# Attention with its gradient: one small turn taken from the DMA queue to TensorE, zero rows stored later, GpSimd's table spread over more steps

## Chip, cores and metric

One core of a Trainium2 chip. The metric is the device time of the whole program in microseconds (us), lower is better. The kernel computes a gated mix of an attention block and a state-space convolution and all its gradients, in bfloat16 with sums in float32.

## The reference, cut to what matters

The forward function is below; the kernel must return its output and the gradients with respect to all inputs but `B_u`, for a given `grad_out` of 1 x 2048 x 576 (32 heads of 18, 2048 positions).

```python
def _A_ref(x, wqkv, wo):
    qkv = (x @ wqkv).reshape(B, S, 3, H, Dh).transpose(2, 0, 3, 1, 4)
    q, k, v = qkv[0], qkv[1], qkv[2]
    scores = jnp.einsum("bhqd,bhkd->bhqk", q, k) * (Dh ** -0.5)
    p = _softmax(scores, axis=-1)
    o = jnp.einsum("bhqk,bhkd->bhqd", p, v)
    return o.transpose(0, 2, 1, 3).reshape(B, S, D) @ wo
...
x = A_x
g = _sigmoid((x * gate_w).sum(-1, keepdims=True))
a = _A_ref(x, A_wqkv, A_wo)
b = _B_ref(x, ...)   # a convolution over the sequence with a kernel made of 128 complex powers per channel
return g * a + (1 - g) * b
```

## The kernel before

The program has four parts: projections and preparations (to about 205 us in the profile), attention forward and backward (to about 2200 us), the convolution part, and the last products. All three parts of the change lie in the attention part.

**Units and steps.** Heads are taken in 8 groups `g` of four, queries in 4 blocks `b` of 512. A pair (g, b) is a *unit*: 32 units, numbered u = 4g + b. A loop over `G` walks through steps, 32 (`NST`) to a unit; below, "step s of unit u" is G = 32u + s. The step range of the forward part is `NTOT` = 1024. The backward part of a unit runs `OFF` = 39 steps behind its forward part: it begins at step 7 of the next unit. So the backward part of a new group begins at step 7 of units 1, 5, 9, ... 29.

**One step.** The order of every engine's instructions is written out by hand in this loop, and each engine runs its own list in order. First come the actions put on record for the step (`at(("pre", G), ...)`: loads and stores). TensorE then makes a pair of score tiles for the forward part (P1), does the "burst" of the step, a pair of score tiles for the backward part (P3), and a pair of products of V with the gradient (P2, named `ps_P<-dOaT,VaT_g` in the profile). ScalarE takes the exponentials of P1 (`PT`, line 780) and of P3 (`eb`, line 785), 128 x 1024 each. VectorE multiplies each P2 tile with its PT into `ds` (line 790).

**Bursts.** They go by `slot`, the place of the step in eight: two steps each for the sums of dV, dQ and dK (`dv_half`, `dq_half`, `dk_half`; the second step of each ends with an addition on VectorE, `gb` when it is the last of its sum), and two slots, 4 and 7, in which `turn_ds` turns blocks of `ds` on TensorE. All bursts share one PSUM bank, `accB`, so a burst waits until VectorE has emptied the one before.

**Turned copies of ds.** dK needs `ds` turned, as `dsT`. For each 128 keys, SyncE issues a DMA transpose for three of the four heads (line 798); the fourth is turned by TensorE and copied by VectorE (lines 561 and 562). `by_pe(p)` says how many of the two tiles of pair p are treated so: none for p = 5, one for p = 6, else both; where TensorE doesn't, the DMA transpose takes all four heads.

**The end of a unit's forward part.** At step 0 of the next unit the sum `accO` is complete and copied (f0, line 500). At step 2 (f1) TensorE turns it, VectorE takes the reciprocals `rl` of the softmax sums and the normalised output `Ob`, and GpSimd scales the gradient with the reciprocals into `dOa` (line 514) and multiplies it with Ob into `prod` (line 516). At step 3 (f2) VectorE reduces prod into the last column of each head's part of `dOa` (line 522), and SyncE stores Ob (line 523) and turns `dOa` into `dOaT` (line 525). P2 reads dOaT from step 7 on, and dV's burst reads dOa.

**SyncE's queue.** It holds all loads of attention, the DMA transposes of ds, dOaT, and those of finished gradients: `store_grad` turns a `gb` into `gT` (line 534), which GpSimd packs and stores (lines 538 and 539). `gb` has two buffers, so the third next sum waits until a gT has landed. In the last unit of a group (b = 3) the sums of dV and dK end for each of the four key blocks, so that eight gT come on top of dQ's one.

**GpSimd.** It builds the table `E_d` of complex powers for the convolution (lines 358 to 420: products of two small tables, stored 144 times by GpSimd's own DMAs) in pieces between its other work. `e_emit(G)` issues as many pieces as `want` says for the step, except in steps 0 and 1 of a unit. It also copies rows of x and of the gated gradient into layouts for the convolution (`put_x`, `put_gy`, every 56 steps from G = 78 and 98), and stores zero rows: one DMA into `Kp_d` at G = 40, and seven (`put_zero`, line 681) into `xb_d` at G = 46, 50, ... 70. The convolution part, after attention, reads all of these.

Of the kernel before, what the change touches and what calls it, by code (L numbers as in the profile page):

```python
# [11 lines left out]
BF = mybir.dt.bfloat16  # L12
# [5 lines left out]
P = 128  # L18


def build(tc, aps, dbg_aps=None, stages=("s1", "attn", "post", "s4", "final")):
    nc = tc.nc
# [39 lines left out]
    with ExitStack() as gctx:  # L62
# [3 lines left out]
        ident_bf = const.tile([P, P], BF, name="ident_bf")  # L66
# [37 lines left out]
        Kp_d = dram.tile([NBLK, 2 * P, CB], BF, name="Kp_d")  # L104
# [11 lines left out]
        with ExitStack() as ctx:  # L116
            s1 = ctx.enter_context(tc.tile_pool(name="s1", bufs=1))
            work = ctx.enter_context(tc.tile_pool(name="s1work", bufs=2))
# [310 lines left out]
        if "attn" in stages:  # L429
            KB = 512  # L430
            NQ = S // KB
            TPQ = KB // P
            DA = HP
            NFILL = {"V": 1, "Q": 0, "K": 0}
            with ExitStack() as ctx:
# [3 lines left out]
                work = ctx.enter_context(tc.tile_pool(name="awork", bufs=2))  # L439
                apsp = ctx.enter_context(tc.tile_pool(name="aps", bufs=1, space=bass.MemoryType.PSUM))  # L440
# [39 lines left out]
                UN = {}  # L480
# [13 lines left out]
                def post_forward(g, b, acc):  # L494
                    U = UN[(g, b)]
                    st = {}

                    def f0():
                        st["oT"] = work.tile([P, KB], F32, tag="oT", bufs=1, name="oT")
                        nc.vector.tensor_copy(st["oT"], acc)  # L500

                    def f1(po):
                        for qi in range(TPQ):
                            nc.tensor.transpose(po[:, qi * P:(qi + 1) * P], st["oT"][:, qi * P:(qi + 1) * P], ident_f)
                        po = po.rearrange("p (t a b) -> p t a b", a=4, b=HP)

                        def ev():
                            rl = work.tile([P, TPQ, 4], F32, tag="rl", bufs=1, name="rl")
                            nc.vector.reciprocal(rl, po[:, :, :, DH])
                            rlb = rl.unsqueeze(3).to_broadcast([P, TPQ, 4, DH])  # L510
                            Ob = st["Ob"] = work.tile([P, TPQ, 4, DH], BF, tag="Ob", bufs=1, name="Ob")
                            nc.vector.tensor_tensor(Ob, po[:, :, :, 0:DH], rlb, op=A.mult)
                            da = U["dOa"]
                            nc.gpsimd.tensor_tensor(da[:, :, :, 0:DH], U["dO"], rlb, op=A.mult)
                            prod = st["prod"] = work.tile([P, TPQ, 4, DH], F32, tag="oT", bufs=1, name="prod")
                            nc.gpsimd.tensor_tensor(prod, da[:, :, :, 0:DH], Ob, op=A.mult)
                        return ev

                    def f2():
                        da, Ob, prod = U["dOa"], st["Ob"], st["prod"]  # L520
                        with nc.allow_low_precision(reason="summed in float32 by the engine, rounded once when written"):
                            nc.vector.tensor_reduce(da[:, :, :, DH], prod, axis=AX.X, op=A.add, negate=True)
                        nc.sync.dma_start(O_d[:, b * TPQ:(b + 1) * TPQ, 4 * g * DH:4 * (g + 1) * DH], Ob.rearrange("p t a b -> p t (a b)"))
                        U["dOaT"] = work.tile([P, TPQ, P], BF, tag="dOaT", name="dOaT")
                        nc.sync.dma_start_transpose(out=U["dOaT"], in_=U["dOa"].rearrange("p t a b -> p (t a b)"))
                    return f0, f1, f2

                def grad_tile():
# [22 lines left out]
                def by_pe(p):  # L551

                    return {NPF: 0, NPF + 1: 1}.get(p, 2)

                def turn_ds(U, p):

                    n = by_pe(p)
                    pt_ = apsp.tile([P, n, TPQ, P], BF, tag="accB", name="dst_p")
                    for x in range(n):
                        for qb in range(TPQ):  # L560
                            nc.tensor.transpose(pt_[:, x, qb, :], U["ds"][2 * p + 2 - n + x][:, 3, qb * P:(qb + 1) * P], ident_bf)  # L561
                    return lambda: nc.vector.tensor_copy(U["dsT", p][:, 2 - n:2, 3 * TPQ:, :], pt_)  # L562

                NPF = 5
                NST = 2 * NT
                NU = NG * NQ
                OFF = NST + 7
                units = [(g, b) for g in range(NG) for b in range(NQ)]
# [3 lines left out]
                def at(n, f):  # L572
                    todo.setdefault(n, []).append(f)

                def accB(name):
                    return apsp.tile([P, KB], F32, tag="accB", name=name)
# [3 lines left out]
                def fill(acc, n, w=4):  # L580
                    o_ = acc[:, (4 - w) * P:4 * P].rearrange("p (a b) -> p a b", b=P)
                    for _ in range(n):
                        mm(o_, lhsT=J_bf, rhs=fill_r[:, 0:w, :])
# [57 lines left out]
                e_total = sum(x[0] for x in eops)  # L641
                e_done = [0.0, 0]

                def e_emit(G):

                    want = (e_total + 270.0) * min(1.0, max(0.0, (G - 10) / (NTOT - 40)))
                    while e_done[1] < len(eops) and e_done[0] < want:
                        e_done[0] += eops[e_done[1]][0]
                        eops[e_done[1]][1]()
                        e_done[1] += 1  # L650
# [15 lines left out]
                NTOT = NU * NST  # L666
# [13 lines left out]
                def put_zero(r):  # L680
                    nc.gpsimd.dma_start(xb_v[:, :, r, :].rearrange("b k w -> k b w"), zrow[:, 0:SUB * CB].unsqueeze(1).to_broadcast([NB, NBLK, SUB * CB]))

                at(("pre", 40), lambda: nc.gpsimd.dma_start(Kp_d[:, 0:P, :].rearrange("b (z u) c -> b z (u c)", z=2),
                                                            zrow.unsqueeze(1).to_broadcast([NBLK, 2, S])))
                for r in range(NSUB - 1):
                    at(("pre", 46 + 4 * r), lambda r=r: put_zero(r))
                for k in range(NT):
                    at(("pre", 78 + 56 * k), lambda k=k: put_x(k))
                    at(("pre", 98 + 56 * k), lambda k=k: put_gy(k))
                for G in range(NTOT + OFF + 24):  # L690
# [4 lines left out]
                    if G < NTOT:  # L695
                        u, s = divmod(G, NST)
                        g, b = units[u]
# [11 lines left out]
                    if r1:  # L709
                        g, b, i, j0 = r1  # L710
# [5 lines left out]
                    evs = []  # L716
                    slot = (G2 + 1) % 8
                    m_ = (G2 - (7, 8, 8, 8, 8, 8, 8, 0)[slot]) // 8
                    if ("f1", G) in todo:
                        acc = accB("accF")  # L720
                        evs.append(todo.pop(("f1", G))[0](acc))
                        e_done[0] += 1.4
                    elif 0 <= m_ < NTOT // 8:
                        u_, kq = divmod(m_, NQ)
                        g, b = units[u_]
                        if slot in SLOTS:
                            nm, burst, h = SLOTS[slot]
                            if h == 0:
                                acc = accB("acc" + nm)
                                fill(acc, NFILL[nm])  # L730
                                burst(g, b, kq, 0, acc)
                            else:
                                evs.append(burst(g, b, kq, 1, acc))
                                if nm == "Q" and kq == NQ - 1:
                                    at(("pre", G + 2), lambda g=g, b=b: store_grad(UN[(g, b)].pop("dqa"), g, 0, b * TPQ))
                                elif nm in "KV" and b == NQ - 1:
                                    at(("pre", G + 2), lambda g=g, kq=kq, nm=nm: store_grad(DKV.pop((nm.lower(), g, kq)), g, 1 + "KV".index(nm), kq * TPQ))
                        elif by_pe(2 * kq + (slot == 4)):
                            evs.append(turn_ds(UN[(g, b)], 2 * kq + (slot == 4)))
                    if r2:  # L740
                        g, b, s2 = r2
                        T = grp_t[g]
                        U = UN[(g, b)]
                        par_ = (s2 + OFF) % 2
                        jo = 2 * par_
                        kq, ii = s2 // 8, (s2 % 8) // 2
# [11 lines left out]
                    if G % 8 in (0, 3, 4, 7) and G >= 3:  # L758
                        i_ = (G - 3) // 8 * 4 + {3: 0, 4: 1, 7: 2, 0: 3}[G % 8]
                        u_, i_ = divmod(i_, NT)  # L760
                        if 0 <= u_ < NU:
                            g, b = units[u_]
# [13 lines left out]
                    for (kind, g, b, i, j, ps) in rows:  # L776
                        U = UN[(g, b)]
# [8 lines left out]
                        else:  # L786
# [6 lines left out]
                            if U["dsn", i] == nj:  # L793
                                p = i // 2
                                assert j == nj - 1
                                if i % 2 == 0:
                                    U["dsT", p] = work.tile([P, 2, 4 * TPQ, P], BF, tag="dsT", bufs=3, name="dsT")
                                nc.sync.dma_start_transpose(out=U["dsT", p][:, i % 2, 0:nj * TPQ, :],
                                                            in_=U["ds"][i][:, 0:nj, :].rearrange("p j q -> p (j q)"))
# [5 lines left out]
                    if G % NST not in (0, 1) or G >= NTOT:  # L805
                        e_emit(G)
# [359 lines left out]
        if "final" in stages and "s4" in stages:  # L1166
# [14 lines left out]
            with ExitStack() as ctx:  # L1181
# [128 lines left out]
                work = ctx.enter_context(tc.tile_pool(name="pbwork", bufs=2))  # L1310
# [5 lines left out]
                for t in range(NT):  # L1316
                    if t % TB == 0:
                        OT4 = work.tile([P, TB, DC, P], BF, tag="OT4", name="OT4")
                        nc.sync.dma_start_transpose(out=OT4.rearrange("p t c q -> p (t c) q"),
                                                    in_=O_tok[:, t:t + TB, :].rearrange("p t d -> p (t d)"))  # L1320
# [100 lines left out]
```

## Time and profile before

| | |
|---|---|
| time, median of three runs | 2997.47 us (2994.35 to 3002.66) |
| span of the profiled execution | 2998.7 us |
| attention: first and last exponential | 205.2 and 2198.3 us |
| exponentials, PT and eb | 1024 each, 128 x 1024 |
| DMA transposes of ds | 512 |
| DMA transposes of dOa | 32, 1.20 us of SyncE each (median) |
| stores of zero rows into xb_d | 7 of 288 KB, at 266.6 to 312.8 us |

How to read it: in the lists of instructions a line has the start in us, the duration in us, the engine, the line of the kernel, the operation, and `out<-in` by the program's names with the shapes; `x2` means two instructions merged. Brackets at the end give the idle time of that engine just before, and what ended it. `SPq` is SyncE's queue of DMA issues, where a duration is that of issuing, not of the transfer. In the table of stretches a row begins with the stretch and its length, and each engine has its busy time. The DMA share is the mean busy share of the 16 DMA engines; where packets overlap it can exceed 1.

### The profile page before, as it was taken

Reading aid. Unit: us, or ns where it says so; the run is one execution under the profiler, and the core shown is the slowest. Engines: PE = TensorE matmul, PEld = TensorE weight load, DVE = VectorE, ACT = ScalarE, POOL = GpSimd, SP = SyncE. Lnnn points to the kernel's source line nnn. Section 1 sums busy time; section 2 is a strip of 40 time slices with the busy share of each in tenths; the row PEclk is TensorE's granted clock in tenths of the full one; section 3 lists DMA queues with packets and bytes.
Section 4 is the critical chain, followed back from the end, with each engine's and each line's share of the span. In section 5 each row is a group of like instructions: output and inputs, shape, how many; then the busy total and the mean of one; then the engine's idle time right before and its main releaser. Section 6 shows DMA issues by size and latency. Waiting matters only on the chain.

```text
span 2998.7 us, 69333 instructions
## 1 busy us (share of the span) xinstructions
PE 2484.7 (83%) x27004; PEld 1188.0 (40%) x27004; DVE 2350.2 (78%) x4115; ACT 2374.2 (79%) x2765; POOL 1606.3 (54%) x2653
## 2 busy tenths in 40 slices
PE   4768888888988888888888898888947878886679
PEld 2432232332333233233233233323226777776447
DVE  4436797898889888898889888988836888889634
ACT  2449898999999899999999999999736777675111
POOL 1038888888888799888888888850010000000010
PEclk8877798999999899999999999999757878887889
DMA  8857999989989989989998999997688887872886
GB/s 223 159 151 123 155 160 164 165 160 168 162 158 164 163 157 167 167 160 161 176 154 164 168 167 154 165 166 127 122 189 215 210 198 207 213 190 72 245 207 130
DMA packets 1310750, 504.17 MB, mean 168 GB/s; under 512 B 1205182, under 2 KB 1280544, under 8 KB 1301204
## 3 DMA queue, kind: packets, MB, share of 16 engines
q1 hardware_dynamic: 1281908, 439.11, 76.5%
q0 software_dynamic: 20624, 53.26, 7.5%
q10 hardware_dynamic: 7888, 7.38, 0.8%
q8 instruction: 211, 3.46, 0.5%
q14 instruction: 119, 0.97, 0.1%
HBM read 144.48 MB, written 99.69 MB: 81 GB/s over the span
## 4 chain that ended last, share of the span: by engine, by line
ACT 35%; PE 23%; DVE 22%; DMA 8%; issue 6%; SPq 3%; POOL 1%; ACTq 0%; DVEq 0%; POOLq 0%
ACT eb L785 20%; ACT PT L780 13%; PE ps_P L30 7%; DVE ds L790 6%; DVE tz L976 3%; DVE tz L979 2%; DVE HG L980 2%; PE accV L30 2%; PE dst_p L561 2%; PE ps_dx L30 2%; PE accK L30 1%; DVE pq L1046 1%; DMA dsT<-ds 1%; PE accO L30 1%; DVE wa L995 1%
## 5 line engine op out<-in xcount | busy, mean ns | idle before, releaser
L790 DVE TENSOR_TENSOR ds<-ps_P,PT 128x512 bf16<-128x512 f32 x2048 | 1312.4, 683 | 169.2 <-PE ps_P L30 131.2
L785 ACT ACTIVATE eb<-ps_P 128x1024 bf16<-128x1024 f32 x1024 | 1098.5, 1073 | 65.6 <-PE ps_P L30 64.4
L780 ACT ACTIVATE PT<-ps_P 128x1024 bf16<-128x1024 f32 x1024 | 1101.3, 1078 | 29.4 <-PE ps_P L30 28.0
L30 PE MATMUL ps_P<-dOaT,VaT_g 32*128 32x512 bf16 x2048 | 577.9, 399 | 50.7 <-DMA dOaT<-dOa 21.3
L358 POOL TENSOR_TENSOR et<-eG,eT 128x448 f32<-128x448 f32 x576 | 542.0, 961 | 10.9
L30 PE MATMUL ps_P<-QaT_g,KaT_g 32*128 32x512 bf16 x2048 | 417.8, 401 | 149.3 <-ACT PT L780 134.1
L30 PE MATMUL ps_P<-KaT_g,QaT_g 32*128 32x512 bf16 x2048 | 416.2, 399 | 6.9 <-ACT eb L785 6.0
L30 PEld LDWEIGHTS <-KaT_g 32*128 32x128 bf16 x2048 | 149.1, 92 | 482.2 <-issue 466.1
L358 POOL TENSOR_TENSOR Eo<-et,et 128x448 bf16<-128x448 f32 x288 | 326.9, 1135 | 20.7
L1082 POOL TENSOR_TENSOR SS<-m 128x96 f32<-128x96 f32 x18 | 9.2, 511 | 557.4 <-ACT m L1080 557.4
L30 PEld LDWEIGHTS <-QaT_g 32*128 32x128 bf16 x2048 | 118.4, 92 | 301.4 <-issue 279.8
L30 PE MATMUL accO<-PT,Vtok_g 128*32 128x512 bf16 x2048 | 216.8, 410 | 0.0
L30 PE MATMUL accV<-eb,dOa 128*32 128x512 bf16 x2048 | 187.8, 400 | 27.4 <-ACT eb L785 27.0
L30 PE MATMUL accK<-dsT,Qtok_g 128*32 128x256 bf16 x4096 | 168.0, 287 | 11.6 <-DMA dsT<-ds 10.6
L30 PE MATMUL accQ<-ds,Ktok_g 128*32 128x512 bf16 x2048 | 167.3, 406 | 2.3 <-DVE gb L600 1.9
L938 ACT COPY E1e<-etp 128x1024 bf16<-128x1024 bf16 x144 | 135.9, 1043 | 22.3 <-PE etp L937 17.0
L562 DVE COPY dsT<-dst_p 128x1024 bf16<-128x1024 bf16 (+1 forms) x224 | 144.3, 644 | 3.9 <-PE dst_p L561 3.8
L561 PE MATMUL dst_p<-ident_bf,ds 128*128 128x128 bf16 x1664 | 139.1, 228 | 5.0 <-DVE gb L618 4.0
L30 PEld LDWEIGHTS <-Vtok_g 128*32 128x32 bf16 x2048 | 53.9, 94 | 224.9 <-issue 223.1
L30 PEld LDWEIGHTS <-E1n 128*128 128x128 bf16 x2304 | 96.7, 109 | 96.8 <-issue 96.4
L30 PE MATMUL yp<-Rw,E1n 128*128 128x30 bf16 x1152 | 67.8, 232 | 79.4 <-DVE Rw L1001 64.8
L561 PEld LDWEIGHTS <-ds 128*128 128x128 bf16 x1664 | 100.0, 101 | 63.6 <-issue 63.5
(244 smaller groups left out, 3678.9 us busy)
## 6 DMA issues: line engine op xcount, KB each, us to landing
E_d<-Eo POOLq DMA_DIRECT2D x144, 256.0 KB, 3.8
E1n<-E_d SPq DMA_DIRECT2D x36, 1024.0 KB
xs<-xb_d SPq DMA_DIRECT2D x18, 1024.0 KB
T0w<-Kp_d SPq DMA_DIRECT2D x18, 1024.0 KB
Md_d<-mst SPq DMA_DIRECT2D x36, 288.0 KB
dsT<-ds SPq DMA_TRANSPOSE x512
dqkv_d<-dtk POOLq DMA_DIRECT2D x96, 72.0 KB, 4.2
QKV_d<-stg SPq DMA_DIRECT2D x12, 504.0 KB
```

The source lines that it names most:

```text
L30: return nc.tensor.matmul(out, lhsT=lhsT, rhs=rhs, start=start, stop=stop, **kw)
L358: nc.gpsimd.tensor_tensor(out, a, b, op=op)
L561: nc.tensor.transpose(pt_[:, x, qb, :], U["ds"][2 * p + 2 - n + x][:, 3, qb * P:(qb + 1) * P], ident_bf)
L562: return lambda: nc.vector.tensor_copy(U["dsT", p][:, 2 - n:2, 3 * TPQ:, :], pt_)
L780: nc.scalar.activation(U["PT"][i, j // 2], ps, ACT.Exp)
L785: nc.scalar.activation(e, ps, ACT.Exp)
L790: nc.vector.tensor_tensor(U["ds"][i][:, j, :], ps, U["PT"][i, j // 2][:, j % 2, :], op=A.mult)
L938: nc.scalar.copy(E_[:, 4 * q:4 * q + 4], pt_)
L976: nc.vector.tensor_tensor(tz, HG[:, :, k - 1, :].unsqueeze(1).to_broadcast([P, 2, 4, CB]), ZZ, op=A.mult)
L979: nc.vector.tensor_tensor(t0v, t0v, UVk[:, :, :, k, :], op=A.add)
L980: nc.vector.tensor_tensor(HG[:, :, k, :].rearrange("p (r s) c -> p r s c", s=2), t0v, t1v[:, ::-1], op=A.add)
L995: nc.vector.tensor_tensor(B_[nm], B_["HG"].rearrange("p q k c -> p (q k) c"), B_["par"][:, r_, :].unsqueeze(1).to_broadcast([P, 4 * NS, CB ...
```

## The change

It has three parts. The DMA transpose of dOa at step 3 goes. In its place TensorE turns the four 128 x 128 blocks of dOa at step 5, in the same burst as the four blocks of ds there (p = 6, a slot 7), and VectorE copies the result from accB into `dOaT`; `turn_ds` becomes a helper `turn` for one or more tiles with one copy for each. For the first unit, step 5 has no other burst. The zero rows are stored at G = 200 (`Kp_d`) and 216, 272, ... 552 (`xb_d`), in place of 40 and 46 to 70. The step at which GpSimd's table reaches its full allowance moves from NTOT - 30 to NTOT + 20: the divisor 984 becomes 1034.

```diff
-                        U["dOaT"] = work.tile([P, TPQ, P], BF, tag="dOaT", name="dOaT")
-                        nc.sync.dma_start_transpose(out=U["dOaT"], in_=U["dOa"].rearrange("p t a b -> p (t a b)"))
                     return f0, f1, f2
...
-                def turn_ds(U, p):
+                def turn(tiles, outs):
+
+                    pt_ = apsp.tile([P, len(tiles), TPQ, P], BF, tag="accB", name="turn_p")
+                    for x, t_ in enumerate(tiles):
+                        for qb in range(TPQ):
+                            nc.tensor.transpose(pt_[:, x, qb, :], t_[:, qb * P:(qb + 1) * P], ident_bf)
+
+                    def ev():
+                        x = 0
+                        for n, o_ in outs:
+                            nc.vector.tensor_copy(o_(), pt_[:, x:x + n])
+                            x += n
+                    return ev
+
+                def ds_tiles(U, p):
 
                     n = by_pe(p)
...
+                    return [U["ds"][2 * p + 2 - n + x][:, 3, :] for x in range(n)], [(n, lambda: U["dsT", p][:, 2 - n:2, 3 * TPQ:, :])]
+
+                def do_tile(U):
+                    U["dOaT"] = work.tile([P, TPQ, P], BF, tag="dOaT", name="dOaT")
+                    return [U["dOa"].rearrange("p t a b -> p (t a b)")], [(1, lambda: U["dOaT"].unsqueeze(1))]
...
-                    want = (e_total + 270.0) * min(1.0, max(0.0, (G - 10) / (NTOT - 40)))
+                    want = (e_total + 270.0) * min(1.0, max(0.0, (G - 10) / (NTOT + 10)))
...
-                at(("pre", 40), lambda: nc.gpsimd.dma_start(Kp_d[:, 0:P, :].rearrange("b (z u) c -> b z (u c)", z=2),
+                at(("pre", 200), lambda: nc.gpsimd.dma_start(Kp_d[:, 0:P, :].rearrange("b (z u) c -> b z (u c)", z=2),
...
-                    at(("pre", 46 + 4 * r), lambda r=r: put_zero(r))
+                    at(("pre", 216 + 56 * r), lambda r=r: put_zero(r))
...
+                    elif G == NST + 5:
+                        evs.append(turn(*do_tile(UN[units[0]])))
...
-                        elif by_pe(2 * kq + (slot == 4)):
-                            evs.append(turn_ds(UN[(g, b)], 2 * kq + (slot == 4)))
+                        else:
+                            p = 2 * kq + (slot == 4)
+                            t_, o_ = ds_tiles(UN[(g, b)], p) if by_pe(p) else ([], [])
+                            if G % NST == 5 and G // NST - 1 < NU:
+                                t2, o2 = do_tile(UN[units[G // NST - 1]])
+                                t_, o_ = t2 + t_, o2 + o_
+                            evs.append(turn(t_, o_))
```

More of the change, by code (lines that the diff above doesn't have):

```diff
@@ L553, in by_pe @@
                     return {NPF: 0, NPF + 1: 1}.get(p, 2)
-                def turn_ds(U, p):
-                    n = by_pe(p)
[L558 to L562, printed above, removed]
+                def turn(tiles, outs):
[10 more added lines that the diff above has]
+                def ds_tiles(U, p):
+                    n = by_pe(p)
+                    return [U["ds"][2 * p + 2 - n + x][:, 3, :] for x in range(n)], [(n, lambda: U["dsT", p][:, 2 - n:2, 3 * TPQ:, :])]
+                def do_tile(U):
+                    U["dOaT"] = work.tile([P, TPQ, P], BF, tag="dOaT", name="dOaT")
+                    return [U["dOa"].rearrange("p t a b -> p (t a b)")], [(1, lambda: U["dOaT"].unsqueeze(1))]
                 NPF = 5
```

## The prediction, made before the result was known

> **What bounds the kernel now.** I read the page first, then the busy time by stretches, then the timelines of single engines around the places where ScalarE stops. The page names no engine that is always full:
>
> ```profile
> PE 2484.7 (83%) x27004; PEld 1188.0 (40%) x27004; DVE 2350.2 (78%) x4115; ACT 2374.2 (79%) x2765; POOL 1606.3 (54%) x2653
> ```
>
> The forward and backward attention (about 205 to 2200 us) is where all parts of the change lie. Busy time by stretches (us, then PE, PEld, DVE, ACT, POOL, each with its count, then TensorE's clock, DMA share, GB/s):
>
> ```profile
> 255.00:320.00 65.00, 55.44 (x521) 17.34 (x518) 49.28 (x81) 55.99 (x60) 60.55 (x96) 0.82 1.07 158
> 609.00:1000.00 391.00, 343.17 (x3637) 118.31 (x3633) 338.98 (x557) 376.65 (x408) 336.85 (x545) 0.96 0.93 164
> 1990.00:2060.00 70.00, 62.63 (x679) 21.55 (x677) 62.65 (x103) 70.00 (x77) 12.10 (x15) 1.00 0.77 137
> ```
>
> ScalarE is full (377 of 391 us; 70 of 70), so its exponentials set the pace. The DMA engines are at 0.93 while GpSimd builds its table, at 0.77 once it is done, and over full in the first stretch, where the zero rows are stored. ScalarE's own timeline shows the pace and one of its stops (unit 9, steps 6 to 8; start, duration, operation, idle time before it):
>
> ```profile
> 739.44 1.07 ACT L785 ACTIVATE eb<-ps_P 128x1024 bf16<-128x1024 f32 x1
> 740.36 1.08 ACT L780 ACTIVATE PT<-ps_P 128x1024 bf16<-128x1024 f32 x1
> 741.39 1.02 ACT L785 ACTIVATE eb<-ps_P 128x1024 bf16<-128x1024 f32 x1
> 746.22 1.02 ACT L780 ACTIVATE PT<-ps_P 128x1024 bf16<-128x1024 f32 x1 [3.81 <-PE ps_P L30]
> 747.73 1.02 ACT L785 ACTIVATE eb<-ps_P 128x1024 bf16<-128x1024 f32 x1 [0.49 <-PE ps_P L30]
> ```
>
> Undisturbed, one exponential starts 0.90 us after the other, 1.81 us a step. The starts of PT 32 apart give a unit: 58.92 us in nearly all (32 x 1.81, and about 1.1 us lost). The exceptions are unit 2 (72.91) and units 5, 9, 13, 17, 21, 25, 29 (67.17, 66.72, 68.14, 66.36, 65.10, 65.18, 65.39), in which a new group's backward part begins. Their excess over 58.92 is 14.0 us and 51.6 us together. In the other units the wait for dOaT costs nothing: step 7, where it is first read, takes 1.95 us there, as do steps 15, 23 and 31, where it isn't new. TensorE at the stop:
>
> ```profile
> 740.90 0.39 PE L30 MATMUL ps_P<-KaT_g,QaT_g 32*128 32x512 bf16 x2
> 744.48 0.61 PE L30 MATMUL ps_P<-dOaT,VaT_g 32*128 32x512 bf16 x2 [3.20 <-DMA dOaT<-dOa]
> 745.57 0.61 PE L30 MATMUL ps_P<-QaT_g,KaT_g 32*128 32x512 bf16 x2
> ```
>
> It waits for dOaT, and afterwards a pair of rows takes 0.61 instead of 0.39 us, for some five steps. The reason is SyncE's queue:
>
> ```profile
> 736.09 1.26 SPq L475 DMA_TRANSPOSE Ktok_g<-QKV_d  x1
> 737.44 1.69 SPq L798 DMA_TRANSPOSE dsT<-ds  x1
> 739.18 0.78 SPq L523 DMA_DIRECT2D O_d<-Ob  x1
> 740.06 2.02 SPq L525 DMA_TRANSPOSE dOaT<-dOa  x1
> 742.17 1.58 SPq L798 DMA_TRANSPOSE dsT<-ds  x1
> 743.81 1.15 SPq L471 DMA_DIRECT2D VaT_g<-QKV_d  x1
> 745.00 0.48 SPq L488 DMA_DIRECT2D dO_b<-dO_d  x1
> 745.58 1.21 SPq L534 DMA_TRANSPOSE gT<-gb  x1
> ```
>
> It issues without a pause. dOa was complete at 735.40 (the reduction at 734.95 takes 0.45), but its turn is issued at 740.06: a queue 4.7 us behind, since at a group's end each gradient of K and V has its own gT. So every later issue is late as well, and this matters below.
>
> **What the Trainium skill says.** "TensorE: Matmul & The Clock Gate", Part 1, has TensorE fall to half its clock after an idle window of about 3.4 us and need as much busy time to return; the slow pairs agree, though unit 21 shows them after a gap of only 0.94 us, so the measured gap counts here. "DMA: Bandwidth & Descriptors", Issuing engines are not separate DMA queues: transfers of all queues share 16 engines. The trace agrees: with GpSimd's zero stores about, TensorE waits 4.86 us for SyncE's dsT (shown below). "VectorE: DVE Perf Modes", The three transpose paths, prices a 128x128 turn at 390 ns on TensorE and 1309 ns by DMA; this trace has 220 ns (median of dst_p) and about 1.2 us of issue for all four blocks, and those I use. The first page's Part 4 says that a turn lands in PSUM and needs a copy.
>
> **The change, part by part.** The sum is against the profiled span, 2998.7 us; the three runs gave 2994.4 to 3002.7, median 2997.5, so 1.2 less.
>
> *1. dOaT leaves SyncE.* Gone are 32 DMA transposes. In plain units nothing waits for them: 0. At the seven group starts ScalarE loses 3.10, 3.81, 5.66, 5.35, 1.11, 3.48, 2.62 us at step 7, 25.1 together. But behind dOaT in the same late queue stands gT of dK (third key block), and DVE's next gb, dQ's last sum at step 9, needs that buffer back. Unit 21, whose first stop was the shortest, shows what comes then; SyncE, then VectorE:
>
> ```profile
> 1476.17 1.85 SPq L534 DMA_TRANSPOSE gT<-gb  x1
> ```
> ```profile
> 1481.72 0.69 DVE L618 SCALAR_TENSOR_TENSOR gb<-accQ,dqa 128x512 bf16<-128x512 f32 x1 [3.24 <-DMA gT<-gb]
> ```
>
> VectorE stands 3.24 us, TensorE's dst_p behind it 2.38, ScalarE 2.37. Without the first stop step 9 comes sooner, gT only by the removed issue (1.25 us; unit 9: 2.06). gT's issues of before are 504.37, 745.58, 990.56, 1235.01, 1476.17, 1718.66, 1961.77. From issue to use took 2.4 to 5.4 us for the seven dOaT and 4.2 and 5.5 for gT in units 29 and 21; mean 4.2. DVE wants gb 4.8 us after step 7 begins (499.9, 740.4, 984.9, 1229.5, 1472.4, 1714.3, 1957.0): 1.95 + 1.81, and 1.05 into step 9. So the new waits are 2.6, 2.5, 3.8, 3.7, 1.9, 2.5, 2.9, together 19.9. Less 0.9 each that the buffers absorb (3.24 against 2.37), ScalarE loses 13.6 in place of 27.5 (25.1, and 2.4 for unit 21's gb): -14. The slow clock takes the rest of the 51.6: 51.6 - 27.5 - 3.5 (step 4's waits for dsT, issued before dOaT and unchanged) = 20.6, or 2.9 a start; most gaps stay near or over 1 us, so I take -1. Together -15. Ends: 0 (gT lands as late as the 5.5, and the clock falls as often) and -45 (no new wait; only step 4's waits and unit 5's slow clock after its own stay).
>
> *2. dOaT on TensorE, step 5.* Four more turns beside the four of ds there: eight take 0.62 us against 0.40, so +0.22 on TensorE; a DVE copy 128x512, 0.42 as the one beside it. Before the turn TensorE must now wait for the reduction; behind it stand the rows of step 5, for which ScalarE and DVE wait. In 31 of 32 units, the next weights of dst_p are loaded 0.92 us or more after the reduction ends, so no wait. The copy delays the ds of step 5 and frees accB 0.42 later for step 6's accV; DVE idles 0.66 in step 6 and TensorE has 0.17 to 0.25 of waits on either side, which hide most. Steps 14, 22, 30, after a full eight-block turn, are 0.12 longer than step 6. I take 0.1 x 32 = +3. Ends: 0 (all hidden; nothing there is removed, so no gain) and 0.64 x 32 = +20.
>
> *3. Zero rows later.* Eight GpSimd DMAs (0.61 us of issue each, 7.2 to landing) leave steps 40 to 70. TensorE at unit 2, step 4:
>
> ```profile
> 304.77 1.04 PE L30 MATMUL accK<-dsT,Qtok_g 128*32 128x256 bf16 x16 [4.86 <-DMA dsT<-ds]
> ```
>
> Again at 326.16 it waits 2.50. No other unit of b = 2 stops, and the loads of group 1 at the same steps have their like in each group; so the overfull engines cause it and unit 2 returns to 58.92: -14. Ends -16 (unit 1's 1.6 too) and -8 (half). In the new places, one in 56 steps (104 us), a store adds little: 0.09 to 0.14 of surplus share over 65 us is 6 to 9 us for all, about 1 us each, 1%. One falls on unit 17, step 8, in a late queue: up to +2. GpSimd's queue past which they move holds table operations only; nothing in attention reads the rows. 0 to +2.
>
> *4. Table spread.* 984 steps become 1034: 5% less table work a step. Table and puts are 0.93 - 0.77 of DMA share, so 0.01 less until step 960, and units 30 and 31 at 0.93 in place of 0.77; these are plain units, which ran without stops at 0.93 before. GpSimd is never waited for but for 7.0 us in three places. The table ends about 2105 us, before its reader after 2200. 0, ends -3 and +3.
>
> Sum: -15 + 3 - 14 + 0 = -26: 2972.7 against the profile, 2971 against the median.
>
> **Rivals.** *A, the wait is gone and nothing follows* (the shorter queue and lighter DMA let gT land in time): -45 - 14 + 3 = -56, 2941. For it: dOaT alone is named at step 7. Against: SyncE issues without a pause to step 12, and unit 21. *B, one of the two gains fails*, by gT taking all of it or by unit 2's stop having another cause: -14 + 3 or -15 + 3, 2985. *C, slower*: TensorE's new wait at step 5. Its slack is 0.92 us; if the reduction came 1.9 us later than now, TensorE would idle 1 us, and the clock fall as in unit 21: 1 + 2.9 us in each of 25 plain units, +98 - 26, 3070. For it: three places where the reduction waited for GpSimd. Against: the same 0.92 in 25 of the 32 units, and GpSimd is less crowded now. That the turn isn't done by TensorE can't be: the DMA line is gone.
>
> **How the numbers follow.** My case 0.60, 2971 (2955 to 2988 from its ends); A 0.15; B 0.17; C 0.08. The range 2940 to 2989 takes in A and B. A measurement can tell about 0.3%, 9 us, from no change. Below 2988.5 lie nearly all of my case, A, and over half of B: 0.83. Within: 0.09. Slower: C, 0.08.
>
> **What would show it.** Right: no DMA named at step 7 of units 5 to 29; a DVE wait of 2 to 4 us for gT at step 9 of most; these units at 62 to 66 us; unit 2 near 59; plain units at 59.0. Wrong: group units near 59 to 61 (A); unit 2 still over 65 (B); plain units over 60 with TensorE waiting for the reduction (C).

## The result, and the profile after

| | before | after |
|---|---|---|
| median, us | 3000.06 (2994.35 to 3005.91, 4 runs) | 2980.34 (2975.94 to 2985.03, 4 runs) |
| span of the profiled execution, us | 2998.7 | 2976.5 |
| mean TensorE clock in that execution | 0.902 | 0.917 |

The ratio of the times is 0.9934, with a 95% interval of 0.9908 to 0.9961: some 20 us gained (12 to 28). Predicted were 2971 us and a range of 2940 to 2989, so the time lies in the range, 9 us above the forecast. A second profiled execution of the changed kernel, made among the experiments, has a span of 2981.6 us. I use it below to tell what repeats. By "group starts" I mean units 5, 9, ... 29, in which a new group's backward part begins; the "excess" of a unit is its length over the 58.92 us of an undisturbed ("plain") one.

The page's first line still shows no full engine. TensorE's busy time fell by 16.5 us though it has 128 instructions more; its mean clock is higher:

```profile
PE 2468.2 (83%) x27132; PEld 1186.9 (40%) x27132; DVE 2359.4 (79%) x4147; ACT 2373.2 (80%) x2765; POOL 1605.9 (54%) x2653
```

Busy time by stretches, columns as before:

```profile
255.00:320.00 65.00, 59.13 (x615) 20.30 (x611) 57.53 (x95) 63.79 (x70) 57.33 (x95) 0.95 0.88 149
609.00:1000.00 391.00, 345.71 (x3645) 119.84 (x3638) 337.78 (x557) 375.40 (x406) 322.26 (x530) 0.95 0.95 161
1990.00:2060.00 70.00, 62.73 (x673) 21.60 (x672) 63.48 (x106) 70.00 (x77) 57.53 (x98) 1.00 0.85 147
```

In the first stretch (unit 2) ScalarE is busy for 63.79 of 65 us where it was 55.99; the DMA share is 0.88 where it was 1.07. In the last, GpSimd now still builds its table, and ScalarE stays full. In the middle nothing was gained: 375.40 against 376.65 us. Unit 9 shows why. ScalarE, VectorE, TensorE and SyncE about the place where ScalarE stopped for 3.81 us before:

```profile
735.13 1.02 ACT L799 ACTIVATE PT<-ps_P 128x1024 bf16<-128x1024 f32 x1
739.23 1.02 ACT L804 ACTIVATE eb<-ps_P 128x1024 bf16<-128x1024 f32 x1 [3.08 <-PE ps_P L30]
```
```profile
736.90 0.69 DVE L630 SCALAR_TENSOR_TENSOR gb<-accQ,dqa 128x512 bf16<-128x512 f32 x1 [3.96 <-DMA gT<-gb]
```
```profile
737.64 1.01 PE L558 MATMUL turn_p<-ident_bf,ds 128*128 128x128 bf16 x8 [3.10 <-DVE gb L630]
738.58 0.61 PE L30 MATMUL ps_P<-KaT_g,QaT_g 32*128 32x512 bf16 x2
```
```profile
733.64 4.29 SPq L817 DMA_TRANSPOSE dsT<-ds  x2
```

The wait for dOaT is gone. At step 9 VectorE, which must write dQ's last sum, waits 3.96 us for a buffer that gT still reads; TensorE's next burst waits for VectorE, ScalarE for TensorE, and the pairs of rows after it take 0.61 us again. SyncE's queue is still late: two turns of ds take 4.29 us to issue. In VectorE's list of waits from 240 to 2125 us this line took the place of TensorE's wait for dOaT (engine, line, releaser; us in total, times, longest):

```profile
DVE gb L630 <- DMA gT<-gb: 32.1, 7, 7.7
```

Where the 22.2 us between the two profiled spans lie (a unit runs from its first PT to the next unit's):

| place | before | after | after, second execution |
|---|---|---|---|
| first PT | 205.2 | 206.1 | 205.9 |
| unit 1 | 54.99 | 55.47 | 55.39 |
| unit 2 | 72.91 | 58.92 | 58.92 |
| group starts, excess | 51.6 | 47.0 | 48.9 |
| ScalarE's loss to the named wait in these units | 27.5 (dOaT, one gT) | 28.6 (gT, seven) | 19.5 (gT, five) |
| the other units from 3 to 30, excess | 1.1 | 3.8 | 4.3 |
| of which unit 12 | 0 | 3.0 | 3.6 |
| last PT to last eb | 73.3 | 67.8 | 70.8 |
| after the last eb | 800.5 | 798.3 | 798.3 |

Unit 2 gives 14.0 us, the seven group starts only 4.6 (2.7), unit 12 costs 3, the end of attention gives 5.4 (2.5), what follows it 2.2 (the kernels below have 797.6 to 804.3 us there, so I don't count that as the change's).

The group starts' sum hardly changed, but its place did. Their excess by steps, in us, from the starts of PT against the medians of plain units; the last two columns are kernels of the next section:

| steps | before | after | after, second execution | turn alone | turn and zero rows |
|---|---|---|---|---|---|
| 4 to 6 | 5.2 | 2.9 | 11.9 | 3.8 | 11.4 |
| 7 to 9 | 36.4 | 2.6 | 0.2 | 0.0 | 3.9 |
| 10 to 12 | 9.7 | 38.8 | 27.8 | 36.1 | 28.0 |
| 13 to 31 | 0.2 | 2.6 | 9.0 | 0.3 | 6.3 |

Steps 7 to 9 follow the wait for dOaT, 10 to 12 the wait for gT, 4 to 6 mostly waits for dsT. The second execution has the same waits of VectorE for gT only at five of the seven group starts:

```profile
DVE gb L630 <- DMA gT<-gb: 21.4, 5, 6.9
```

There units 13 and 21 had already stopped at step 4, where TensorE waited 3.08 and 2.38 us for dsT. So which transfer of the late queue is waited for differs between executions of one kernel, and the sum (47.0 and 48.9) much less.

### The profile page after: what moved, and what is told of

It reads as the page before. It is cut to its first block, busy times and chain, and to the rows that moved or that the text cites. A ratio compares the mean times of both kernels' runs of the same rounds, so it can differ in the third digit from the quotient of the medians.

```text
span 2976.5 us, 69573 instructions
## 1 busy us (share of the span) xinstructions
PE 2468.2 (83%) x27132; PEld 1186.9 (40%) x27132; DVE 2359.4 (79%) x4147; ACT 2373.2 (80%) x2765; POOL 1605.9 (54%) x2653
## 4 chain that ended last, share of the span: by engine, by line
ACT 34%; DVE 23%; PE 21%; DMA 8%; issue 7%; POOL 4%; SPq 3%; ACTq 0%; DVEq 0%; POOLq 0%
ACT eb L804 20%; ACT PT L799 13%; PE ps_P L30 7%; DVE ds L809 7%; DVE tz L995 3%; DVE HG L999 2%; DVE tz L998 2%; PE accV L30 2%; DMA gT<-gb 2%; PE turn_p L558 2%; PE ps_dx L30 2%; DVE pq L1065 2%; PE ps_dwq L30 1%; POOL et L358 1%; PE accK L30 1%
## 5 line engine op out<-in xcount | busy, mean ns | idle before, releaser
L30 PE MATMUL ps_P<-dOaT,VaT_g 32*128 32x512 bf16 x2048 | 581.4, 390 | 32.8 <-DVE ds L809 18.3
L358 POOL TENSOR_TENSOR et<-eG,eT 128x448 f32<-128x448 f32 x576 | 542.0, 961 | 10.7
L30 PE MATMUL ps_P<-KaT_g,QaT_g 32*128 32x512 bf16 x2048 | 408.5, 391 | 2.2 <-ACT eb L804 1.6
L558 PE MATMUL turn_p<-ident_bf,ds 128*128 128x128 bf16 x1664 | 137.3, 227 | 29.9 <-DVE gb L630 28.8
L30 PE MATMUL accQ<-ds,Ktok_g 128*32 128x512 bf16 x2048 | 159.2, 388 | 3.2 <-DVE gb L612 2.6
L563 DVE COPY dsT<-turn_p 128x1024 bf16<-128x1024 bf16 (+1 forms) x224 | 144.2, 644 | 4.9 <-PE turn_p L558 4.9
L30 PE MATMUL yp<-Rw,E1n 128*128 128x30 bf16 x1152 | 67.8, 232 | 83.5 <-DVE Rw L1020 69.0
```

The costliest lines, as they stand in the source:

```text
L30: return nc.tensor.matmul(out, lhsT=lhsT, rhs=rhs, start=start, stop=stop, **kw)
L358: nc.gpsimd.tensor_tensor(out, a, b, op=op)
L558: nc.tensor.transpose(pt_[:, x, qb, :], t_[:, qb * P:(qb + 1) * P], ident_bf)
L563: nc.vector.tensor_copy(o_(), pt_[:, x:x + n])
```

## The experiments

Each kernel was timed beside the kernel before on the same chip; ratios are to that kernel. 0.001 is 3 us.

**One part alone.** The first three kernels carry one part of the change each.

*Turn alone* (the changed kernel with the last two parts undone):

```diff
-                    want = ... (G - 10) / (NTOT + 10) ...
+                    want = ... (G - 10) / (NTOT - 40) ...
-                at(("pre", 200), ... Kp_d ...
+                at(("pre", 40), ... Kp_d ...
-                    at(("pre", 216 + 56 * r), lambda r=r: put_zero(r))
+                    at(("pre", 46 + 4 * r), lambda r=r: put_zero(r))
```

> The kernel before with the first part alone: dOa turned by TensorE at step 5, zero rows and table as before. My theory (a late SyncE queue; the wait moves from dOaT to gb; the zero rows alone fill the DMA engines in unit 2): no DMA wait at step 7 of the group starts, a VectorE wait for gT of 2 to 7 us at step 9 of nearly all of them, these seven units 45 to 51 us over plain ones together (51.6 before), unit 2 still over 68 us; in all 0 to 7 us faster. Rival (the turn also cures unit 2, since one transfer less stands in the full queue): unit 2 under 62 us and 12 to 20 us faster. Rival (the wait for dOaT was worth its 25 us): group starts under 30 us over plain units.

Measured: 0.9963 (0.9951 to 0.9975), 11 us gained. The seven group starts fell from 51.6 to 40.1 us of excess, and VectorE waits for gT at step 9 of all seven (29.5 us together). Unit 2 fell to 64.42: of its two waits of TensorE for dsT, 4.86 and 2.50 us, one was left, 4.08. The group starts gained more than this run's expectation allowed (45 to 51) and less than the 15 us of the prediction, and unit 2, which I had at over 68, gained 8.5.

*Zero rows alone* (the kernel before with one part):

```diff
-                at(("pre", 40), ... Kp_d ...
+                at(("pre", 200), ... Kp_d ...
-                    at(("pre", 46 + 4 * r), lambda r=r: put_zero(r))
+                    at(("pre", 216 + 56 * r), lambda r=r: put_zero(r))
```

> The kernel before with the second part alone: zero rows stored at steps 200 and 216 to 552. My theory: unit 2 at 58.9 us (72.9 before), the group starts' waits for dOaT as before, two of the new places cost something (the store at the start of unit 12 about 3 us by a late dsT, the one in unit 17 about 2 to 4 us); in all 7 to 13 us faster, half or more of the whole change. Rival (unit 2's stop is of another make, the dOaT transpose in the full queue): unit 2 still over 66 us, no gain.

Measured: 0.9978 (0.9968 to 0.9987), 7 us. Unit 2 is back to 58.94, the 14 us expected. Unit 17, where a zero row is stored at step 8, grew from 66.36 to 70.82, and unit 12, where one is stored at step 0, stops for 1.4; the group starts together are nearly unchanged (52.7). The profiled execution is 14.2 us shorter than that of before, so it doesn't show where the typical run gives back the other 7.

*Table alone* (the kernel before with one part):

```diff
-                    want = ... (G - 10) / (NTOT - 40) ...
+                    want = ... (G - 10) / (NTOT + 10) ...
```

> The kernel before with the third part alone: divisor NTOT + 10 for GpSimd's table. My theory: within 3 us of the kernel before, the same waits at the same steps. Rival (the lighter DMA load a step is what shortened the tail and the group starts): 6 us or more faster, with the seven group starts under 46 us over plain units together.

Measured: 0.9952 (0.9937 to 0.9967), 14 us. I had this part at nothing. In its profiled execution (2989.5 us; its runs go from 2974.7 to 2996.9) unit 2 has lost 5.2 us and the group starts 5.8. Either GpSimd must be waited for after all, or its DMAs. The three gains alone make 32 us, and together 20. The next kernels ask for the reasons.

**What the table's part does.** Two theories: fewer of GpSimd's stores at a time, or a GpSimd less full. More stores, the same GpSimd work (kernel before; every fourth stored piece of the table is stored once more, into a scratch that nothing reads):

```diff
-                            nc.gpsimd.dma_start(E_d[:, q:q + EH], Eo.pop(q))
+                            nc.gpsimd.dma_start(E_d[:, q:q + EH], Eo[q])
+                            if (q // EH) % 4 == 0:
+                                nc.gpsimd.dma_start(E2_d[:, q:q + EH], Eo[q])
```

> The kernel before, with every fourth store of GpSimd's table issued a second time, into a scratch tensor: 36 more stores of 256 KB, a quarter more table traffic on the DMA engines (their share up by about 0.02), GpSimd 21 us busier (1%). It asks why the table's slower pace alone, which I had at nothing, made the kernel 14 us faster. Theory a (the DMA engines: 5% fewer stores a step shorten every late transfer): 15 us slower or more. Theory b (GpSimd itself: its lists are shorter at a unit's end): 2 to 6 us slower, no more. Theory d (only where the stores fall against the group starts changed): anything within 8 us, with no order in it.

Measured: 1.0029 (1.0019 to 1.0039), 9 us lost; the group starts have 63.0 us of excess in place of 51.6. That lies between what the theories said. The longer group starts agree with what the Trainium skill says in "DMA: Bandwidth & Descriptors", Issuing engines are not separate DMA queues: DMAs run on the same 16 engines whichever engine starts them. The transfers alone are not shown to be the cause, since issuing 36 more also takes GpSimd some 21 us (36 at 0.59 us, the mean of its table stores). In any case a quarter more table stores for 9 us doesn't make 14 us out of 5% less.

Less work, the same stores (kernel before; one of the two large products of every piece of the table is left out):

```diff
-                    eops.append((1.02, lambda mul=mul, ri=ri, st=st: mul(1, 1 - ri, st)))
+                    eops.append((1.02, lambda st=st: st.append(st[0])))
```

> The kernel before, with one of the two large products of every table piece left out (the table is not the reference's): the same stores at the same steps, GpSimd some 270 us less busy. Theory b (a crowded GpSimd delays dOa, prod and the packing of gT, whose buffers SyncE waits for): 12 us faster or more. Theory a (the DMA engines alone): within 4 us of the kernel before. Theory d: within 8 us.

Measured: 0.9953 (0.9937 to 0.9969), 14 us: the whole gain of the table's part, with all its stores in place. The group starts are at 47.3, unit 2 at 63.23. VectorE's products into ds take 683 ns each in the mean here, before and with the faster table below, and 684 with the table's part alone, so a lighter GpSimd doesn't make them shorter.

A faster table (kernel before; the other direction, by as many steps):

```diff
-                    want = ... (G - 10) / (NTOT - 40) ...
+                    want = ... (G - 10) / (NTOT - 90) ...
```

> The kernel before, with the table's divisor 934 in place of 984: 5% more table work a step, the opposite of the change's third part. Theories a and b (more of it at a time costs, less gains): 8 to 16 us slower. Theory d (where the pieces fall): no slower than 5 us, or even faster. Under a theory that the gain comes from the last units' cold or warm clock and not from the pace: within 5 us.

Measured: 1.0068 (1.0051 to 1.0084), 20 us lost, and in another place: units 6, 10, 16, 19 and 24, plain before, take 62.5 to 65.0 us (28.3 us of excess outside unit 2 and the group starts). The group starts are at 44.5, lower than before: so their lower values with the table's part alone (45.8) and with less work (47.3) are no evidence for what a lighter GpSimd does there. VectorE's wait for `prod` in the three kernels, from 240 to 2125 us (faster, before, changed):

```profile
DVE dOa L522 <- POOL prod L516: 34.6, 14, 7.1
```
```profile
DVE dOa L522 <- POOL prod L516: 7.0, 3, 4.4
```
```profile
DVE dOa L522 <- POOL prod L516: 1.1, 1, 1.1
```

Its counterpart is GpSimd's own wait for the reciprocals at step 2, its reserve: 86.2 us in 9 of 32 units with the faster table, 126.0 in 27 before, 180.8 in all 32 after. One of the new stops (unit 10; VectorE, then TensorE, with the faster table):

```profile
802.35 0.46 DVE L522 TENSOR_REDUCE dOa<-prod 128x16 bf16<-128x288 f32 x1 [3.53 <-POOL prod L516]
```
```profile
803.45 0.58 PE L561 MATMUL dst_p<-ident_bf,ds 128*128 128x128 bf16 x4 [3.27 <-DVE dkacc L632]
803.97 0.61 PE L30 MATMUL ps_P<-KaT_g,QaT_g 32*128 32x512 bf16 x2
```

GpSimd was near an edge: with 5% more table work a step the whole kernel loses 20 us, and with 5% less (1.1 us with the table's part alone, too) the 7.0 us are nearly gone. They are not the whole of the 14 us. The longest of before is in unit 2, at step 4:

```profile
304.47 0.46 DVE L522 TENSOR_REDUCE dOa<-prod 128x16 bf16<-128x288 f32 x1 [4.40 <-POOL prod L516]
```

TensorE's wait of 4.86 us for dsT, shown in the prediction, ends 0.3 us after it; with the table's part alone VectorE no longer waits there, and TensorE still does, for 4.97 us.

**Whether the parts add up** (the changed kernel with the table's part undone, by its one line):

```diff
-                    want = ... (G - 10) / (NTOT + 10) ...
+                    want = ... (G - 10) / (NTOT - 40) ...
```

> The changed kernel with the third part taken back (divisor 984): turn and zero rows alone. If the three parts' gains (11, 7 and 14 us alone) added up this would be 18 us faster than the kernel before, and the whole change 32; since the whole gives 20, theory of one shared stock (each part relieves the same late queue at the same group starts): 14 to 20 us faster than the kernel before, hardly behind the changed kernel. Theory that the parts harm each other elsewhere (new stops in units 12 and 17): as fast as or faster than the changed kernel, without stops in unit 12.

Measured: 0.9937 (0.9920 to 0.9953), as much as the whole change. Turn and zero rows add up (11 + 7 alone, 19 together); the table adds nothing that can be measured to both. Part of that is one shared stock: unit 2 and the next group start, unit 5, have together 22.2 us of excess before, 12.0 with the turn alone, 5.2 with the zero rows, 14.2 with the table, 5.7 with the first two, 5.6 with all. What one part has taken there, another can't. The 7.0 us of waits for `prod` are shared likewise: 1.9 with the zero rows alone, whose stores no longer stand in GpSimd's list in unit 2, and 1.8 here.

**The wait for gT.** The third buffer for dQ's last sum is that of `oT`, which is free at that time (changed kernel):

```diff
-                            o_ = U["dqa"] = grad_tile()
+                            o_ = U["dqa"] = work.tile([P, KB], BF, tag="oT", bufs=1, name="gq")
```

> The changed kernel, with dQ's last sum written into the buffer that oT and prod use (free at that step) in place of gb, so that nothing waits for the gT of dK at step 9. My theory (that wait is what remains of the group starts): no wait for gT at step 9, the seven group starts 5 to 20 us over plain units together (47 in the changed kernel), 25 to 42 us faster than the changed kernel, 0.977 to 0.985 of the kernel before. Rival (the late queue itself sets the length of these stretches, so that the next transfer, dsT at step 12 or the next gb, takes over): 0 to 12 us faster than the changed kernel, with a DMA wait at step 11 or 12 in its place.

Measured: 0.9919 (0.9899 to 0.9939). The wait of VectorE for gT is gone, and the group starts fell from 47.0 to 33.3 us, not to the 5 to 20 of my theory. TensorE now waits for dsT, from the same late queue: at step 12 in units 5, 17, 25 and 29, and at step 4 or 20 in the others. In the list of waits, 240 to 2125 us, and at the worst place, unit 17:

```profile
PE accK L30 <- DMA dsT<-ds: 21.2, 12, 4.6
```
```profile
1220.37 6.72 SPq L817 DMA_TRANSPOSE dsT<-ds  x2
```
```profile
1229.15 1.04 PE L30 MATMUL accK<-dsT,Qtok_g 128*32 128x256 bf16 x16 [4.60 <-DMA dsT<-ds]
```

The same buffer in the kernel before, by the same edit:

> The kernel before with dQ's last sum in the buffer of oT in place of gb, and nothing else. If the two waits stand one behind the other, as I hold (dOaT at step 7 hides gT at step 9): the seven waits for dOaT stay, only those of units 21, 25 and 29 for gb go, 2 to 7 us faster. If gb's buffers were the deeper cause (they hold SyncE's queue up even before): 12 us or more.

Measured: 0.9981 (0.9970 to 0.9991), 6 us, about the 5.6 us of waits for gT that this takes away. Five waits of 3.05 to 4.82 us for dOaT are left at step 7, and units 21 and 25 have next to none. The group starts are at 40.9 us, 10.7 lower; as this is one execution, I don't read more into it.

**The zero rows' new places.** The kernel with the free buffer and the zero rows in the middle of plain units, clear of group starts and of step 0; beside it, the changed kernel once more:

```diff
-                    at(("pre", 216 + 56 * r), lambda r=r: put_zero(r))
+                    at(("pre", 32 * (6, 7, 8, 10, 11, 14, 15)[r] + 18), lambda r=r: put_zero(r))
```

> The changed kernel with dQ's last sum in the buffer of oT, and the seven zero stores at step 18 of units 6, 7, 8, 10, 11, 14 and 15, where no unit begins and no group's backward part. Theory (the store at unit 12, step 0 and the one in unit 17 cost 3 and 2 to 4 us): unit 12 at 58.9, no stop of a plain unit, 8 to 16 us faster than the changed kernel. Rival (a store costs the same wherever it falls, since the DMA engines are full): 3 to 9 us, as much as the freed gb alone, with stops in other units.

> The changed kernel itself, once more, beside the three below on one chip: 0.991 to 0.996 of the kernel before.

Measured: 0.9877 (0.9856 to 0.9898), median 2964.3 us, against 0.9937 (0.9915 to 0.9960), 2981.85 us, for the changed kernel: the best of all versions. Its interval lies clear of the changed kernel's, and only just below that of the free buffer alone (0.9898 against 0.9899, on two chips), so the part of the zero rows in it is small and not firmly shown. Unit 12 no longer stops and unit 17 is at 62.12 (65.21 with the free buffer alone). Against that unit 9 takes 72.63 us, the longest group start of all profiles (67.09 with the free buffer alone), and I don't know why; the group starts together are at 35.8, not lower. The long wait for gT at unit 17 in the changed kernel repeats (7.67 and 6.88 us, and 6.42 without the table's part; 3.62 in the one execution with the turn and the zero rows early), so a zero row at step 8 comes with 3 to 4 us more there. Unit 12 stops in four of the five profiles that have a zero row at its step 0 (not in the one without the table's part).

Last, two more loads off the late moments (this best version, with Ob stored from GpSimd's queue and the table spread by 20 more steps):

```diff
-                        nc.sync.dma_start(O_d[...], Ob...)
+                        nc.gpsimd.dma_start(O_d[...], Ob...)
-                    want = ... (G - 10) / (NTOT + 10) ...
+                    want = ... (G - 10) / (NTOT + 30) ...
```

> As the one above, and the store of Ob moved from SyncE's queue to GpSimd's (0.9 us of SyncE a unit), and the table's divisor 1054. Theory (SyncE's late queue is what remains: waits for dsT at steps 12 and 20 of the group starts): those waits shorter by about 1 us each, group starts 5 to 12 us shorter together than without it, 4 to 12 us faster. Rival (the DMA engines' fill sets the lateness, whoever issues): within 3 us.

Measured: 0.9888 (0.9866 to 0.9910), 2970.3 us, not better, so my theory fails. The group starts gained 3.0 us (35.8 to 32.8), but the stretch after the last PT took 76.1 in place of 67.6. Which of the two edits did that is open.

## Why the prediction was right, and where it wasn't

**The sum came out near, but not from its terms.** Predicted were -26 us, measured -22 in the profile and -20 in the runs. Unit 2 came as forecast. That the rest is near is luck: the group starts gave some 10 us less than forecast and unit 12 lost 3, while the turn's 3 us on TensorE did not come and the end of attention and what follows it, not in the forecast, were 7.6 us shorter (4.7 in the second execution).

*1, the turn leaves SyncE: -15 predicted, -4.6 found (-2.7 in the second execution).* The mechanism was right as far as it went: no DMA of dOaT is named anywhere, and gT takes its place at step 9, at seven group starts in the first execution and at five in the second. (One DMA is named at step 7: in unit 13 VectorE waits 0.89 us for an earlier gT.) The working for the new wait was, for each start, gT's issue plus 4.2 us to use, less the time at which VectorE wants the buffer. On average over the seven, against the beginning of step 7:

| | predicted | measured | second execution |
|---|---|---|---|
| gT issued | 3.5 us | 3.9 | 2.5 |
| issue to use | 4.2 | 4.9 | 5.0 (the five) |
| VectorE wants gb | 4.8 | 4.2 | 4.0 (the five) |
| waits for gT, sum | 19.9 | 32.1 | 21.4 |
| ScalarE's loss behind them, sum | 13.6 | 28.6 | 19.5 |

Two terms of the sum were mis-sized. The first is the wait for gT itself. VectorE came 0.6 us earlier than I had counted, and gT took 0.7 longer than my mean; both repeat. The 4.9 could have been had from the trace of before: in the three units where VectorE did wait for gT there (21, 25 and 29) it took 5.5, 5.0 and 4.2 us, and I mixed them with dOaT's times. The buffers absorb 0.5 us a start in the first execution (32.1 against 28.6), where I had 0.9. Only in the first execution does this make the wait much longer than forecast; in the second gT was issued 0.9 us earlier than forecast, and the sum of the waits came out as predicted.

The second is the rest of the queue. I left the waits for dsT at step 4 "unchanged" and put nothing behind gT. In the second execution steps 4 to 6 lose 11.9 us (5.2 before) and steps 13 to 31 lose 9.0 (0.2), together 15.4 more than in the first, while steps 7 to 12 lose 13.4 less. The same is seen without the table's part (11.4 and 6.3). So the queue's lateness costs these units 47 to 50 us in all three executions that have the turn and the late zero rows, however it is shared among dsT and gT. With the turn alone they lost 40.1; how much of the difference is the zero rows', beyond unit 17, is open. How much of the excess is the slow clock was not measured apart.

*2, the turn on TensorE: +3 predicted, nothing found.* Steps 5, 6 and 7 of plain units have the same medians before and after (1.81, 1.82 and 1.95 us), and the units take 58.92. The slack beside it hides all of it. TensorE's wait for the reduction did not come, as the 0.92 us of slack had said, but for 1.1 us in two places.

*3, zero rows: -14 predicted, -14.0 found at unit 2.* With the zero rows alone it is the same, so this term stands. The overfull DMA engines were not all of unit 2's stop, as I had it: VectorE waited 4.40 us for GpSimd at the same step. The price of the new places was too low: 0 to +2 was allowed for unit 17 alone. Unit 12 costs 3.0 more, and unit 17 some 3 to 4 of the wait booked under 1.

*4, the table: 0 predicted.* By itself that is refuted: 14 us alone, 14 us with less GpSimd work and all stores, 20 us lost in the other direction. My reason was that GpSimd is "never waited for but for 7.0 us in three places"; it counted waits that had happened, and not how near the others were. Within the whole change the part is worth nothing measurable, since the other two lighten the same places. How GpSimd's load makes up the rest of the 14 us is not settled. A queue of gradients held up by GpSimd's packing doesn't show: in the profile SyncE's issue of gT waits some 34 us for GpSimd before and as much with the table's part alone.

*Not foreseen:* the end of attention. It took 73.3 us before, 67.8 and 70.8 in two executions of the changed kernel, 68.3 with turn and zero rows, 71 to 74 in the kernels with one part. It differs by 3 us between executions of one kernel and was 67.6 to 76.1 in the later kernels, so it isn't plainly the change's. The stretch from 2110 to 2178 us, before and after:

```profile
2110.00:2178.00 68.00, 61.40 (x532) 19.05 (x527) 58.97 (x98) 43.68 (x46) 4.92 (x8) 0.67 0.69 124
```
```profile
2110.00:2178.00 68.00, 54.40 (x559) 17.46 (x557) 64.01 (x108) 41.24 (x41) 8.46 (x14) 0.94 0.80 144
```

TensorE's clock was 0.67 there before and 0.94 after. Why is argued only: at the same point TensorE idles for the same time in both (last section).

**The rivals.** A, no wait after dOaT's, is refuted: the group starts take 62 to 69 us. Even with gT's wait removed they keep 33.3 us of excess, and dsT is the next in the queue that is waited for; A's 2941 wasn't reached by any version. B, one of two gains fails, comes closest for the place: the turn's gain was mostly taken by gT and dsT, and its 2985 is 5 us from the median, my own 2971 nine. C, slower by TensorE's wait for the reduction, did not come with the change. With the faster table its like did: VectorE waits for `prod`, TensorE behind it, the clock falls, and 20 us are lost. It was a real edge, on the far side of what the change did.

## What to carry to other kernels

Where an in-order queue is late, taking out the wait that is named brings forward the next one from the same queue (here dOaT, then gT, then dsT): price the whole row of them, each with its own time from issue to use, and look at a second execution before saying which one costs what. Background work has an edge that the waits of before don't show: look at the reserve of the engine that does it, in how many units it still waits for its input, and place its stores where no queue is late. Effects of parts measured alone need not add up when they relieve the same places.

## What the hardware showed that I had not expected

A gap of less than 1 us on TensorE can come with the slow rows (0.61 us a pair), or without them. At the end of attention TensorE waits 0.83 us for the same instruction; before, then after:

```profile
2129.99 0.90 PE L504 MATMUL accF<-ident_f,oT 128*128 128x128 f32 x4 [0.83 <-DVE dqa L618]
2130.82 0.61 PE L30 MATMUL ps_P<-KaT_g,QaT_g 32*128 32x512 bf16 x2
```
```profile
2115.44 0.66 PE L504 MATMUL accF<-ident_f,oT 128*128 128x128 f32 x4 [0.83 <-DVE dqa L630]
2116.03 0.39 PE L30 MATMUL ps_P<-KaT_g,QaT_g 32*128 32x512 bf16 x2
```

The same four products take 0.90 us in one and 0.66 in the other, and the pairs after them 0.61 and 0.39. Issuing a DMA transpose of ds takes SyncE 1.27 us at the least and 1.56 in the median before, but up to 6.50. At unit 17's group start one took 4.01 us in the changed kernel and 5.17 with the free buffer (the next one 1.45 in both):

```profile
1221.96 4.01 SPq L817 DMA_TRANSPOSE dsT<-ds  x1
```

Its ds had been complete for 7 us, and in the kernels before and after all 512 have ds complete before their issue begins, so this is not a wait for the input: the issuing itself is slowed, not only the landing. By what is not shown.
